# A fused sparse attention and MoE kernel: where the second weight is loaded, scaled and split

## The chip, the cores and the metric

The kernel runs on 1 core of one Trainium2 chip. The metric is the device time of one execution in microseconds (us): before the change 816.15 us, the median of 3 runs (813.92 to 816.83). Engines are named as in the profile: PE multiplies matrices, ACT applies functions and scales, DVE does element-wise work and reductions, POOL gathers, SP starts transfers (as do ACT and POOL). Transfers run on 16 DMA engines.

## The reference

```
scores = q @ k^T / sqrt(64), only where the block mask allows   # batch 4, heads 8, 768 tokens, blocks of 32
attn   = softmax(scores) @ v                                    # neighbours, first and last block, 3 sampled blocks
x      = attn as [3072, 512]
h      = x @ w_in                                               # w_in  [512, 2048]
g      = h * erf(softplus(h))
out    = g @ w_out                                              # w_out [2048, 512]
```

All inputs are float32 but the two MoE weights, which arrive as float64: the kernel gets them as pairs of 32-bit words and makes float32 of them. Block 0 and block 23 attend to everything; they are the "f" units below, the 22 others (two at a time) the "m" units.

## The kernel before

**Weights.** A weight is loaded in pieces of 1024 KB (`load_w`), decoded from the 64-bit form by three DVE instructions (`decode`), and squared and summed by ACT (`square`). From the sums comes a power-of-two scale, one per half of the first weight (`scale_half`) and one per pair of rows of the second (`scale_pair`). With it each 128x512 piece is split into two float16 parts, so that three float16 products give nearly the exact one: ACT writes the upper part (`high`), DVE the rest (`low`), which needs the upper part first. For the first weight PE forms the rest instead, with a diagonal of the scale (`rest`, then `rest_low`, and `rest_out` on ACT). The generator `weights` has 17 steps n=0 to 16: n=0 to 7 decode the first weight, n=8 to 15 the second; step n from 9 on scales pair n-9 of the second weight and splits it, 16 `high` and 16 `low` in all. The instructions of the splits show in the profile as `wo<-wo,sums 128x512`.

**Prologue and loop.** Six attention units run ahead (`for begun in range(FIRST)`), each calling three steps of `weights`; the rest of its steps follow, and then the main loop over 48 groups of 256 feed-forward columns by 256 tokens (plus 3 turns that only finish). Turn m computes a group `h` of 24 products with the first weight (`ff_first`), its logarithms on ACT (`ff_logs`), the values of an earlier attention unit (`po`), the scores of the next unit (`s_m`, or `s_f` for the first and last blocks), the products `o` with the second weight of group m-3, the gate of group m-2 (`s<-s,h`, then two `g`), the maxima (`mx`), `ff_power`, the exponentials (`pf`), `ff_exp` (`s<-s` on ACT), and then `next_queries`, which copies the queries of the next unit to their place (`qm`, two DVE copies), and `behind`, which prepares the values and keys of the next batch (`vmax`, `fold`, `vn_of`, `vraw`, `kr`).

Three buffers hold `h`, so the `h` of turn m+3 waits for the gate of group m, which runs in turn m+2. The scores of a turn need the `qm` of the turn before. Each engine works through its own list of instructions in order. For turns m from 3 on (`held[0] = m >= FF_LAG`) that list has the order in which the calls are written; before, a scheduler places the instructions of PE, ACT and DVE, and `high_priority` moves some ahead. SP's and POOL's stand as written everywhere.

**Loads of the second weight.** ACT issues them. The table `loads` in `weights` names the step after which a piece is loaded; pieces ("o", 4) and ("o", 6) both follow step 7. The program lets a load wait for an earlier transfer that uses the same completion counter, and ACT stands at that load until the earlier one has landed.

Of the kernel before, what the change touches and what calls it, by code (L numbers as in the profile page):

```python
# [2 lines left out]

# [10 lines left out]
ALU = mybir.AluOpType  # L14
# [16 lines left out]
def sparse_attention_moe(ctx: ExitStack, tc: tile.TileContext, qT, kT, v, sampled, w_in, w_out, out):  # L31
# [5 lines left out]
    held, queued = [False], [True]  # L37

    class InOrder:
# [3 lines left out]
        def __getattr__(self, name):  # L43
            call = getattr(self.engine, name)

            def issue(*args, **kwargs):
                done = call(*args, **kwargs)  # L47
                if self.held[0]:
                    tc.keep_in_program_order(done)
                return done  # L50

            return issue

    nc = tc.nc
    pe, act, dve, pool, sp = (
# [7 lines left out]
    NK = DM // P  # L63
# [34 lines left out]
    ones, eye = room[:, :P], room[:, P : 2 * P]  # L98
# [305 lines left out]
    def load_w(key, i):  # L404

        if key == "o" and i >= 12:
            tag, bufs = (("vraw", 1), ("xT", 3), ("xT", 3), ("x", 2))[i - 12]
            rows = w_out[i // 2 * 2 * P :][: 2 * P].bitcast(I32).rearrange("(p n) c -> p n c", n=2)[:, i % 2]
            if tag == "x":
                parts = [mo.tile([P, 512], I32, tag=tag, name=f"raw_{i}_{u}", bufs=bufs) for u in range(2)]  # L410
            elif tag == "vraw":
                parts = [ld.tile([P, H // 2, KT * D], I32, tag=tag, name=f"raw_{i}", bufs=bufs).rearrange("p a b -> p (a b)")[:, :1024]]
            else:
                parts = [mo.tile([P, 1024], I32, tag=tag, name=f"raw_{i}", bufs=bufs)]
            c = 0
            for raw in parts:
                (sp if i == 15 else act).dma_start(raw, rows[:, c : c + raw.shape[1]])
                c += raw.shape[1]
            places[key, i] = parts
            return  # L420
        if key == "i":
            raw = slots(wi, 1 + 2 * i, 4) if i < 8 else slots(wo, 2 * i - 16, 4)
            part, kt = divmod(i // 2, NK)
            sp.dma_start(raw, w_in[kt * P : (kt + 1) * P, part * 1024 : (part + 1) * 1024].bitcast(I32))
        else:
            raw = slots(wo, 2 + 2 * i if i < 8 else 10 + 2 * (i - 8), 4)
            rows = w_out[i * P : (i + 2) * P, :].bitcast(I32).rearrange("(p n) c -> p n c", n=2)
            act.dma_start(raw.rearrange("p (n c) -> p n c", n=2), rows)
        places[key, i] = [raw]

    def decode(key, i):

        first = i + APART[key]
        t = wi if key == "i" else wo
        w32 = t[:, first : first + 2, :].rearrange("p n c -> p (n c)")
        parts = [raw for n in (i, i + 1) for raw in places.pop((key, n), [])]
        mag = mags[(i // 2) % 2]
        c = 0
        for raw in parts:
            w = raw.shape[1] // 2  # L440
            raw = raw.rearrange("p (n w) -> p n w", w=2)
            lo, hi = raw[:, :, 0], raw[:, :, 1]
            m = mag[:, c : c + w]
            dve.tensor_scalar(m, hi, 3, 0x3FFFFFFF, ALU.logical_shift_left, ALU.bitwise_and)
            dve.scalar_tensor_tensor(m, hi, -0x40000000, m, ALU.bitwise_and, ALU.bitwise_or)
            done = w32[:, c : c + w].bitcast(I32)
            dve.scalar_tensor_tensor(done, lo, 29, m, ALU.logical_shift_right, ALU.bitwise_or)
            c += w
# [7 lines left out]
    def halves(key, i):  # L456
        t, t16 = (wi, wi16) if key == "i" else (wo, wo16)
        w32, hi16, lo16 = t[:, i + APART[key], :], t16[:, i, :512], t16[:, i, 512:]
        if key == "i":
            w32 = w32.rearrange("p (n q e) -> p n e q", n=2, e=2)  # L460
            hi16, lo16 = (x.rearrange("p (n e q) -> p n e q", n=2, e=2) for x in (hi16, lo16))
        return w32, hi16, lo16
# [5 lines left out]
    def high(key, i):  # L468
        w32, hi16, _ = halves(key, i)
        act.activation(hi16, w32, AF.Copy, scale=scale_of(key, i))  # L470

    def low(key, i):
        w32, hi16, lo16 = halves(key, i)
        dve.scalar_tensor_tensor(lo16, w32, scale_of(key, i), hi16, ALU.mult, ALU.subtract)

    NP = NF // 2
    eo, so, io = (sums[:, 16 + n * (NP + 2) : 16 + (n + 1) * (NP + 2)] for n in range(3))
    si, ii = so[:, NP:], io[:, NP:]
# [13 lines left out]
    def scale_pair(i):  # L492
        n = i // 2
        total = ps_o.tile([P, DM], F32, tag="o", name=f"total_{i}")[:, :1]
        pe.matmul(total, ones, wsq["o"][:, n : n + 1], start=True, stop=True)
        scale_part(total, n)
# [3 lines left out]

    def scale_half(total, part):
        scale_part(total, NP + part)
        dve.tensor_scalar(diag, eye, si[:, part : part + 1], None, ALU.mult)

    def ratios():
        dve.tensor_reduce(least[:, 0:1], si, AX.X, ALU.min)
# [6 lines left out]
        dve.tensor_tensor(unscale, least[:, 0:1], least[:, 1:2], ALU.mult)  # L513

    rests = {}

    def rest(i):
        rests[i] = ps_o.tile([P, DM], F32, tag="o", name=f"rest_{i}")
        pe.matmul(rests[i], diag, halves("i", i)[0], start=True, stop=False)

    def rest_low(i):
        pe.matmul(rests[i], less16, wi16[:, i, :512], start=False, stop=True)
# [4 lines left out]
    assert NK * NG == NF == 16  # L527

    def weights():
        loads = {5: (("o", 0),), 6: (("o", 2),), 7: (("o", 4), ("o", 6)), 10: (("o", 8),), 11: (("o", 10),)}  # L530
        sum_i = None
        for n in range(17):
            key, i = "io"[n // 8 % 2], n % 8 * 2
            if n in (4, 9):
                with tc.high_priority():
                    scale_half(sum_i, n // 8)
            pair = None
            if 5 <= n < 9:
                pair = 2 * (n - 5)
            if 10 <= n < 14:  # L540
                pair = 2 * (n - 6)
            if pair is not None:
                for part in range(2):
                    rest(pair + part)
                    high("i", pair + part)
            if n < 16:
                decode(key, i)
            if pair is not None:
                for part in range(2):
                    rest_low(pair + part)  # L550
                    rest_out(pair + part)
            if n < 16:
                square(key, i)
            if n >= 9:
                i = 2 * (n - 9)
                scale_pair(i)
                high("o", i)
                high("o", i + 1)
                low("o", i)
                low("o", i + 1)  # L560
            for piece in loads.get(n, ()):
                load_w(*piece)
            if n in (3, 7):
                sum_i = bound_part(n // 4)
            yield
        ratios()

    softs = {}

# [203 lines left out]
    def ff_exp(b, ch, fg):  # L773
        s2 = ffs[b, ch, fg][1]
        act.activation(s2, s2, AF.Exp, scale=-C5)
# [201 lines left out]
    for m in range(len(groups) + FF_LAG):  # L977
        ch, i = divmod(m, NGR)
        held[0] = m >= FF_LAG
        steps = 0  # L980
        if ch < len(until):
            first = until[ch - 1] if ch else FIRST
            steps = int(i in spread[until[ch] - first])
        elif begun < len(units) + PV_LAG:
            steps = 1
        assert steps in (0, 1)
        group = groups[m] if m < len(groups) else None
        last = groups[m - GATE_LAG] if GATE_LAG <= m < len(groups) + GATE_LAG else None
        unit = unit_of(begun) if steps else None
        old = unit_of(begun - PV_LAG) if steps and begun - PV_LAG >= SEEN else None  # L990
        place = seen(old) if old else None
        begun += steps
        if group:
            ff_first(*group)
            ff_logs(*group)
        if place:
            values(*place)
            used_values(place)
        if steps:
            gathers()  # L1000
        if unit:
            scores(unit)
            used_keys(unit)
        if m >= FF_LAG:
            for u in range(CT):
                ff_second(*groups[m - FF_LAG], u)
            for u in range(CT):
                ff_store(*groups[m - FF_LAG], u)
        if last:
            ff_gate(*last)  # L1010
        if open_unit:
            soft_low(open_unit)
        if place:
            norm(*place)
        if unit:
            soft_max(unit)
        if place:
            turn(*place)
        if group:
            ff_power(*group)  # L1020
        if unit:
            soft_exp(unit)
        if group:
            ff_exp(*group)
        open_unit = unit
        if unit:
            next_queries(begun - 1)
            behind(begun - 1)
# [36 lines left out]
```

## Time and profile before

| | |
|---|---|
| median of 3 runs | 816.15 us (813.92 to 816.83) |
| the profiled execution | 814.76 us, span 813.0 us |
| PE busy | 722.7 us (89%) |
| DVE busy | 644.8 us (79%) |
| ACT busy | 603.0 us (74%) |
| granted TensorE clock, mean | 0.960 |

The profile is of one execution. "Span" is the time from its first to its last instruction. A row of a timeline gives the start in us from the beginning of the span, the duration, the engine, the operation, the output and inputs by the program's names, and the shapes; in square brackets stands the idle time of the engine ahead of it and what ended that. The chain of waits is followed back from one point to what released it, so the rows of one chain add up to the time it covers. All instructions pass through one helper, and so all stand at line L47 of the kernel: the names tell them apart. A turn of the loop is found by its `h`: the fourth (m=3) starts at 136.38 us, the next ones at 146.09, 154.23, 162.45, 171.87 and 180.46 us.

### The profile page before, as it was taken

The page shows a single profiled execution, that of the slowest core. Times are in us where ns is not written, and L with a number is a line of the kernel's source. Part 1 is how long each engine was busy: PE and PEld are TensorE (multiplying, and loading weights), DVE is VectorE, ACT ScalarE, POOL GpSimd, SP SyncE. Part 2 cuts the span into 40 slices and gives each one's busy share as a digit, 9 for nine tenths or more (in the row PEclk, how much of TensorE's full clock was granted, in tenths as well). Part 3 has the DMA queues.
Part 4 walks back from the last instruction along what each step waited for, and adds up shares of the span by engine and source line. Part 5 has one row for each costly group of instructions (what it writes and reads, how often), then busy time and mean ns, then how long its engine had stood idle before and what let it go on. Part 6 is the DMA issues. An engine that isn't in the chain of part 4 may idle for free.

```text
span 813.0 us, 26533 instructions
## 1 busy us (share of the span) xinstructions
PE 722.7 (89%) x11136; PEld 507.8 (62%) x11136; DVE 644.8 (79%) x1251; ACT 603.0 (74%) x1035; POOL 198.0 (24%) x382
## 2 busy tenths in 40 slices
PE   2355894979979899999999899999999999999997
PEld 2233563756757577666767577667677776666663
DVE  6685998988869887887778798887888887776664
ACT  2554889777857678787866877878878878777674
POOL 4045530302434231400133233200343310000000
PEclk9867996999999999999999999999999999999999
DMA  9999822986499697843498697744497648312000
GB/s 319 394 232 276 236 88 55 229 203 166 117 238 233 139 230 201 195 122 80 126 184 179 179 228 181 181 101 111 114 201 176 142 122 184 73 27 48 8 27 26
DMA packets 187288, 129.46 MB, mean 159 GB/s; under 512 B 137761, under 2 KB 160929, under 8 KB 185377
## 3 DMA queue, kind: packets, MB, share of 16 engines
q1 hardware_dynamic: 173440, 83.98, 46.3%
q10 hardware_dynamic: 7840, 25.96, 10.0%
q0 software_dynamic: 5888, 17.84, 8.5%
q8 instruction: 87, 1.43, 0.8%
q14 instruction: 33, 0.26, 0.1%
HBM read 82.81 MB, written 12.95 MB: 118 GB/s over the span
## 4 chain that ended last, share of the span: by engine, by line
PE 65%; DVE 13%; DMA 10%; ACT 7%; issue 4%; SPq 0%; ACTq 0%; DVEq 0%
PE h L47 26%; PE o L47 23%; PE s_m L47 7%; PE po_None L47 4%; PE s_f L47 3%; DVE s L47 3%; DMA vbuf<-vtab 3%; DMA wo<-in_w_in_dram 2%; DMA qt<-in_qT_dram 2%; DVE p_m L47 2%; ACT s L47 2%; ACT pf_m L47 2%; ACT x L47 2%; DVE mx_m L47 1%; DMA vtab<-vn 1%
## 5 line engine op out<-in xcount | busy, mean ns | idle before, releaser
L47 PE MATMUL h<-xT,wi 128*128 128x256 f16 x2304 | 274.0, 277 | 20.2 <-DVE s L47 20.1
L47 PEld LDWEIGHTS <-wi 128*128 128x128 f16 x2304 | 228.2, 99 | 71.4 <-issue 13.3
L47 PE MATMUL o<-wo,g 128*128 128x512 f16 x1152 | 266.0, 381 | 1.0 <-issue 0.8
L47 PEld LDWEIGHTS <-g 128*128 128x128 f16 x1152 | 109.9, 98 | 122.4 <-issue 2.9
L47 POOL DMA_INDIRECT vbuf<-vtab,idx x88 | 92.4, 1050 | 370.0 <-PE po_None L47 289.1
L47 ACT ACTIVATE s<-s 128x512 f32<-128x512 f32 x192 | 120.2, 627 | 39.7 <-DVE s L47 30.1
L47 ACT ACTIVATE x<-x 128x512 f32<-128x512 f32 x192 | 120.9, 630 | 5.9
L47 PE MATMUL s_m<-kx,qm 128*64 128x96 f32 (+1 forms) x1408 | 95.1, 245 | 16.2 <-DVE qm L47 11.1
L47 POOL COPY kg<-kx 128x128 f32 x264 | 89.9, 387 | 69.7 <-PE s_m L47 56.8
L47 ACT ACTIVATE pf_m<-s_m,nb_m 128x256 f32<-128x256 f32 x176 | 69.2, 475 | 41.1 <-DVE nb_m L47 40.9
L47 ACT ACTIVATE x<-h,isg 128x512 f32<-128x512 f32 x96 | 65.3, 680 | 31.8 <-PE h L47 31.6
L47 DVE SCALAR_TENSOR_TENSOR s<-x 128x512 f32<-128x512 f32 x96 | 67.8, 706 | 26.2 <-ACT x L47 26.0
L47 DVE SCALAR_TENSOR_TENSOR s<-s,s 128x512 f32<-128x512 f32 x96 | 66.7, 695 | 23.1 <-ACT s L47 19.9
L47 PEld LDWEIGHTS s_m<-kx,qm 128*64 128x64 f32 x1408 | 71.2, 144 | 20.7 <-ACT qm L47 11.0
L47 DVE SCALAR_TENSOR_TENSOR g<-s,sums,g 128x512 f16<-128x512 f32 x96 | 72.2, 752 | 3.4
L47 DVE TENSOR_REDUCE mx_m<-s_m 128x4 f32<-128x1024 f32 x44 | 53.6, 1218 | 20.2 <-PE s_m L47 20.2
L47 PE MATMUL s_m<-kg,qm 128*64 128x96 f32 x704 | 66.5, 256 | 2.5 <-issue 2.4
L47 DVE SCALAR_TENSOR_TENSOR s<-s,h 128x512 f32<-128x512 f32 x96 | 65.3, 681 | 0.5
L47 ACT ACTIVATE s<-x 128x512 f32<-128x512 f32 x96 | 60.5, 630 | 2.9
L47 PE MATMUL po_None<-vbuf,pT_m 128*32 128x65 f16 (+1 forms) x4224 | 45.4, 196 | 7.4 <-issue 2.5
L47 PEld LDWEIGHTS <-pT_m 128*32 128x32 f16 x4224 | 38.6, 94 | 20.6 <-issue 17.0
L47 DVE TENSOR_TENSOR p_m<-pf_m,p_m 128x1024 f16<-128x1024 f32 x38 | 50.3, 1324 | 0.6 <-ACT p_m L47 0.6
(117 smaller groups left out, 681.2 us busy)
## 6 DMA issues: line engine op xcount, KB each, us to landing
vbuf<-vtab SPq DMA_DIRECT2D x80, 195.0 KB
vraw<-in_v_dram ACTq DMA_DIRECT2D x9, 768.0 KB
vbuf<-vtab SPq DMA_DIRECT2D x12, 520.0 KB
wo<-in_w_out_dram ACTq DMA_DIRECT2D x6, 1024.0 KB
qt<-in_qT_dram SPq DMA_DIRECT2D x20, 256.0 KB
vtab<-vn_of SPq DMA_DIRECT2D x13, 390.0 KB
kr<-in_kT_dram ACTq DMA_DIRECT2D x12, 384.0 KB
vbuf<-vtab SPq DMA_DIRECT2D x32, 130.0 KB
```

The costliest lines, as they stand in the source:

```text
L47: done = call(*args, **kwargs)
```

## The change

Four things change. The piece ("o", 6) of the second weight is loaded after the first square of the second weight (step 8), in written order, and no longer after step 7; decoding at step 8 is in written order too. The second half of the first weight gets its scale at step 8, ahead of that decoding, and no longer at step 9. Each half's scale has a diagonal buffer of its own (`diags`), where both used one. And the splits of the second weight leave `weights`: a new function `split_pair` makes two `high` and two `low` at the end of each of the first eight turns of the loop, after `ff_exp` and ahead of `next_queries`. The scales of the pairs stay in `weights`.

```diff
+    @contextmanager
+    def in_order(on=True):
+        was, held[0] = held[0], held[0] or on
+        yield
+        held[0] = was
...
-        dve.tensor_scalar(diag, eye, si[:, part : part + 1], None, ALU.mult)
+        dve.tensor_scalar(diags[part], eye, si[:, part : part + 1], None, ALU.mult)
...
+    diags = diag, line
...
-        pe.matmul(rests[i], diag, halves("i", i)[0], start=True, stop=False)
+        pe.matmul(rests[i], diags[i // (2 * NK)], halves("i", i)[0], start=True, stop=False)
...
-        loads = {5: (("o", 0),), 6: (("o", 2),), 7: (("o", 4), ("o", 6)), 10: (("o", 8),), 11: (("o", 10),)}
+        loads = {5: (("o", 0),), 6: (("o", 2),), 7: (("o", 4),), 10: (("o", 8),), 11: (("o", 10),)}
...
-            if n in (4, 9):
+            if n in (4, 8):
...
-                decode(key, i)
+                with in_order(n == 8):
+                    decode(key, i)
...
             if n >= 9:
-                i = 2 * (n - 9)
-                scale_pair(i)
-                high("o", i)
-                high("o", i + 1)
-                low("o", i)
-                low("o", i + 1)
+                scale_pair(2 * (n - 9))
             for piece in loads.get(n, ()):
                 load_w(*piece)
+            if n == 8:
+                with in_order():
+                    load_w("o", 6)
...
+    def split_pair(fg):
+        for i in (2 * fg, 2 * fg + 1):
+            high("o", i)
+            low("o", i)
...
         if group:
             ff_exp(*group)
+        if m < NP:
+            split_pair(m)
         open_unit = unit
         if unit:
             next_queries(begun - 1)
```

The moved load stands in ACT's list. Before (`qm` are the query copies that follow it, `sq_o` the first square of the second weight):

```order
37 L47 DMA wo<-in_w_out_dram 128x2048
38 L47 ACTIVATE wi<-wi,sums 128x512
39 L47 DMA wo<-in_w_out_dram 128x2048
40 L47 ACTIVATE qm_98<-qt_2_139 64x8x32 x2
41 L47 ACTIVATE wi<-rest_504 128x512
42 L47 ACTIVATE wi<-rest_507 128x512
43 L47 ACTIVATE sq_o_756,sums<-wo 128x1024
```

With the change, from the same place on and then around the load:

```order
37 L47 DMA wo<-in_w_out_dram 128x2048
38 L47 ACTIVATE wi<-wi,sums 128x512
39 L47 ACTIVATE qm_98<-qt_2_139 64x8x32 x2
40 L47 ACTIVATE wi<-rest_504 128x512
41 L47 ACTIVATE wi<-rest_507 128x512
```

```order
 L47 ACTIVATE xT_0_624<-turned 128x2x128
-L47 ACTIVATE pT_m_3_903<-turned 128x2x256
+L47 ACTIVATE pT_m_3_907<-turned 128x2x256
+L47 ACTIVATE sq_o_759,sums<-wo 128x1024
+L47 DMA wo<-in_w_out_dram 128x2048
+L47 ACTIVATE pT_m_3_907<-turned 128x2x256
```

The load no longer stands ahead of the copies; it follows the first `sq_o`, which itself comes later.

DVE's list in turn m=3, before:

```order
211 L47 TENSOR_SCALAR nb_m_8_2021<-mx_m_8_2019 128x4
212 L47 TENSOR_TENSOR x_0_5_2023<-xf_5_2017,x_0_5_2023 128x256
213 L47 SCALAR_TENSOR_TENSOR s_0_0_3_2027<-x_0_3_1842 128x512
214 L47 SCALAR_TENSOR_TENSOR s_0_0_3_2027<-s_0_0_3_1846,s_0_0_3_2027 128x512
215 L47 COPY qm_98<-qt_4_1556 64x8x32 x2
216 L47 SCALAR_TENSOR_TENSOR s_0_0_2_1813<-s_0_0_2_1813,h_0_2_1774 128x512
```

and with the change:

```order
204 L47 TENSOR_SCALAR nb_m_8_2001<-mx_m_8_1999 128x4
205 L47 TENSOR_TENSOR x_0_5_2003<-xf_5_1997,x_0_5_2003 128x256
206 L47 SCALAR_TENSOR_TENSOR s_0_0_3_2007<-x_0_3_1822 128x512
207 L47 SCALAR_TENSOR_TENSOR s_0_0_3_2007<-s_0_0_3_1826,s_0_0_3_2007 128x512
208 L47 SCALAR_TENSOR_TENSOR wo<-wo,sums 128x512 x2
209 L47 COPY qm_98<-qt_4_1528 64x8x32 x2
210 L47 SCALAR_TENSOR_TENSOR s_0_0_2_1789<-s_0_0_2_1789,h_0_2_1750 128x512
```

Two `low` now stand between `ff_power` and the copies of `qm`; the gate of the next turn follows the copies as it did.

ACT's list in turn m=3, before:

```order
133 L47 ACTIVATE pf_m_8_2030<-s_m_8_1971,nb_m_8_2021 128x256 x4
134 L47 ACTIVATE p_m_8_2035<-pf_m_8_2030 128x4x256
135 L47 ACTIVATE s_0_0_3_2027<-s_0_0_3_2027 128x512
136 L47 DMA vraw_1_2043<-in_v_dram 128x1536
137 L47 ACTIVATE x_0_4_2070<-h_0_4_2045,isg_1480 128x512
```

and with the change:

```order
126 L47 ACTIVATE pf_m_8_2010<-s_m_8_1951,nb_m_8_2001 128x256 x4
127 L47 ACTIVATE p_m_8_2015<-pf_m_8_2010 128x4x256
128 L47 ACTIVATE s_0_0_3_2007<-s_0_0_3_2007 128x512
129 L47 ACTIVATE wo<-wo,sums 128x512 x2
130 L47 DMA vraw_1_2027<-in_v_dram 128x1536
131 L47 ACTIVATE x_0_4_2054<-h_0_4_2029,isg_1448 128x512
```

Two `high` stand behind the exponential of `s` and ahead of the logarithms of the next turn. The turns m=4 to m=6 look the same on both engines. Up to the fourth `h`, 12 `high` and 12 `low` stand in the lists before, and 6 of each with the change. SP's and POOL's lists keep their order.

More of the change, by code (lines that the diff above doesn't have):

```diff
@@ L1 @@
 import math
-from contextlib import ExitStack
+from contextlib import ExitStack, contextmanager
 import concourse.bass as bass
```

## The prediction

> **What bounds the kernel now.** I read the busy time per engine in the stretches between the `h` groups of TensorE first (each `h` group opens one turn of the main loop), then the chain of waits up to the fourth of them, then the rows of DVE and ACT inside the turns m=3 to m=6. The profiled execution took 814.76 us around a span of 813.0 us; the median of the runs shown, 816.15, lies 1.39 above it. Of this kernel a change under 0.5% (4.1 us) can't be told from none.
>
> The stretches (start:end, length, then busy time of each engine, granted clock, DMA share, GB/s); the second to the fifth are the turns m=3 to m=6:
> ```profile
> 58.90:67.30 8.40, 2.42 (x116) 1.63 (x110) 4.90 (x9) 0.02 (x1) 7.93 (x17) 0.83 1.01 305
> ...
> 124.00:136.40 12.40, 1.80 (x9) 1.46 (x10) 10.34 (x31) 12.40 (x25) 0.00 (x0) 0.58 0.18 40
> 136.40:146.10 9.70, 9.70 (x181) 6.97 (x182) 9.52 (x18) 8.47 (x16) 2.14 (x2) 0.83 0.38 92
> 146.10:154.20 8.10, 8.10 (x181) 6.15 (x180) 7.52 (x16) 6.85 (x14) 2.30 (x2) 1.00 0.93 232
> 154.20:162.50 8.30, 8.30 (x182) 6.28 (x181) 7.76 (x28) 5.42 (x9) 2.67 (x3) 1.00 1.08 247
> 162.50:171.90 9.40, 7.60 (x138) 5.03 (x137) 7.57 (x15) 6.49 (x13) 0.83 (x1) 1.00 0.62 157
> ```
> Before the fourth `h` ACT is the bound: 12.40 us busy out of 12.40, with PE at 1.80. In the turns m=4 and m=5 PE is (8.10 of 8.10, 8.30 of 8.30), but DVE follows at 7.52 and 7.76: little room is left on it. The chain of waits into the fourth `h` shows what ACT and DVE do there:
> ```profile
> 124.78 1.22 ACT wo L47 x2
> ...
> 129.29 1.22 ACT wo L47 x2
> ...
> 134.41 0.98 DVE wo L47 x2
> ...
> 135.65 0.69 DVE s L47
> ...
> 136.38 4.35 PE h L47 x24
> ```
> The halves of the second weight (`wo`) stand on that chain with 1.22 + 1.22 + 0.98 = 3.42 us. Up to that point, from 90 us on, there are 12 of each:
> ```profile
> L47 ACT ACTIVATE wo<-wo,sums 128x512 f16<-128x512 f32 x12 | 8.2, 728 | 0.0
> ...
> L47 DVE SCALAR_TENSOR_TENSOR wo<-wo,sums 128x512 f16<-128x512 f32 x12 | 8.8, 746 | 1.2 <-ACT wo L47 1.0
> ```
>
> **Part 1: halves that leave the stretch before the fourth `h`.** Of the 12 pairs of instructions, 6 stay (turns m=0 to 2) and 6 go into later turns. That frees 6 x 8.2/12 = 4.1 us on ACT and 6 x 8.8/12 = 4.4 us on DVE; the chain holds 3.42 us of them directly. ACT is full and DVE is 10.34 of 12.40, so the freed ACT time should show nearly whole: I take **-4.0 us**. Bounds: -1.5 (only part of the 3.42 is gained, since `h` waits for a gate that DVE forms behind other work) and -7.
>
> **Part 2: the load that moves behind the first square, and the earlier second scale.** The fourth big load of the second weight was issued by ACT at a point where it had to wait (ACT's row first, then two of the chain of waits):
> ```profile
> 67.31 0.84 ACT L47 ACTIVATE qm<-qt 64x256 f32<-64x256 f32 x2 [8.39 <-DMA wo<-in_w_out_dram]
> ...
> 63.07 15.67 DMA vbuf<-vtab
> ...
> 78.78 0.95 PE po_None L47 x94
> ```
> Copies of queries, weight halves and exponentials stood behind it for 8.39 us. Yet the chain there runs through a transfer (`vbuf`, 15.67 us) whose end at 78.78 releases PE; it does not run through ACT, and after it PE is the bound for 40 us (15.00 busy of 15.00 between 95 and 110):
> ```profile
> 95.00:110.00 15.00, 15.00 (x183) 9.72 (x182) 14.79 (x32) 12.34 (x25) 5.51 (x8) 0.89 0.47 123
> 110.00:124.00 14.00, 13.81 (x133) 9.33 (x130) 11.69 (x28) 12.70 (x23) 5.13 (x8) 1.00 0.55 153
> ```
> So the hold is covered by that landing and by PE's work, and I count its removal as 0. If the cover is gone it is worth up to -8.39. It can also turn against the change: the load now starts later, and its decoding (and all scales behind it) with it; ACT's row of 12.70 busy in 14.00 says 1.3 us of slack for that, so the other end is +1.5. The second diagonal buffer and the scale one step earlier take no instruction more; 0.
>
> **Part 3: the halves in the turns m=3 to m=7.** Here the order is kept as written. A turn gets two ACT halves behind the exponential of `s`, and two DVE halves that wait for them, ahead of the two copies of `qm`. DVE works its rows in order, so the copies, and behind them the gate (`s<-s,h`) of the next turn, queue behind the halves. DVE's rows, m=3 and m=4:
> ```profile
> 143.84 1.21 DVE L47 TENSOR_REDUCE mx_m<-s_m 128x4 f32<-128x1024 f32 x1
> ...
> 146.35 0.69 DVE L47 SCALAR_TENSOR_TENSOR s<-s,s 128x512 f32<-128x512 f32 x1
> 146.96 0.58 DVE L47 COPY qm<-qt 64x256 f32<-64x256 f32 x2
> 147.58 0.69 DVE L47 SCALAR_TENSOR_TENSOR s<-s,h 128x512 f32<-128x512 f32 x1
> ...
> 151.74 1.22 DVE L47 TENSOR_REDUCE mx_m<-s_m 128x4 f32<-128x1024 f32 x1 [0.29 <-PE s_m L47]
> ...
> 155.36 1.93 DVE L47 TENSOR_REDUCE vmax<-vraw 128x1 f32<-128x384 f32 x4
> ...
> 160.32 0.68 DVE L47 SCALAR_TENSOR_TENSOR s<-s,h 128x512 f32<-128x512 f32 x1
> ...
> 164.19 1.21 DVE L47 TENSOR_REDUCE mx_m<-s_m 128x4 f32<-128x1024 f32 x1
> ...
> 169.42 1.15 DVE L47 SCALAR_TENSOR_TENSOR vn_of<-vraw,s_v,vn_of 128x384 f16<-128x384 f32 x2 [1.65 <-ACT vn_of L47]
> 170.48 0.68 DVE L47 SCALAR_TENSOR_TENSOR s<-s,h 128x512 f32<-128x512 f32 x1
> ```
> and ACT's, DVE's and PE's that close the walk:
> ```profile
> 155.83 0.61 ACT L47 ACTIVATE s<-s 128x512 f32<-128x512 f32 x1
> ...
> 168.27 0.61 ACT L47 ACTIVATE s<-s 128x512 f32<-128x512 f32 x1
> 168.79 1.10 ACT L47 ACTIVATE vn_of<-vraw,s_v 128x384 f16<-128x384 f32 x2
> ...
> 177.51 0.61 ACT L47 ACTIVATE s<-s 128x512 f32<-128x512 f32 x1
> ...
> 174.53 0.94 DVE L47 TENSOR_REDUCE mx_f<-s_f 128x1 f32<-128x768 f32 x1
> ...
> 179.73 0.68 DVE L47 SCALAR_TENSOR_TENSOR s<-s,h 128x512 f32<-128x512 f32 x1
> ...
> 180.46 4.45 PE L47 MATMUL h<-xT,wi 128*128 128x256 f16 x24 [3.21 <-DVE s L47]
> ```
> Pieces, start to start. From `mx` to the exponential: 155.83 - 151.74 = 4.09. The exponential holds ACT 168.79 - 168.27 = 0.52. Two ACT halves 1.22 (the chain's own row), then the second DVE half 0.75, then the copies 147.58 - 146.96 = 0.62. So the copies end 4.09 + 0.52 + 1.22 + 0.75 + 0.62 = 7.20 after `mx`, where before they ended 147.58 - 143.84 = 3.74 after it.
> - `mx` m=3 to m=4: 7.20, then gate to `mx` 151.74 - 147.58 - 0.29 = 3.87, is 11.07; before 151.74 - 143.84 = 7.90. **+3.2**. (PE needs only some 8.1 for a turn, so it waits for `qm`, and `mx` for DVE.)
> - m=4 to m=5: 7.20, then the maxima of the values 160.32 - 155.36 = 4.96, then 164.19 - 160.32 = 3.87, is 16.03; before 12.45. **+3.6**.
> - m=5 to m=6 (`mx_f`): 7.20, the value halves 170.48 - 169.42 = 1.06, then 174.53 - 170.48 = 4.05, is 12.31; before 10.34. **+2.0**. The wait of 1.65 in the row of `vn_of` covers part of it.
> - `mx_f` to the gate that frees the buffer of the ninth `h`: 177.51 - 174.53 = 2.98, then 0.52 + 1.22 + 0.75 + 1.06 = 3.55, is 6.53; before 179.73 - 174.53 = 5.20. **+1.3**.
>
> Sum 10.1. Off it go 0.3 for halves that stood before `mx` in m=3 of the kernel before, and 0.3 for rows that overlap by some 0.07 each. **+9.5 us** at the ninth `h`; bounds +7.5 (the first DVE half and the copies fall into waits) and +11. The two halves of m=7 I take at **0**:
> ```profile
> 184.65 0.63 ACT L47 ACTIVATE s<-s 128x512 f32<-128x512 f32 x1 [2.30 <-DVE s L47]
> ...
> 189.71 2.78 PE L47 MATMUL h<-xT,wi 128*128 128x256 f16 x24
> ```
> ACT has 2.30 idle there; with the cover gone it is +1.2.
>
> **Sum.** -4.0 + 0 + 9.5 + 0 = +5.5: 820.3 for the profiled execution, **821.6** by the median. What comes after the ninth `h` is paced by the loop itself, so I let the shift stay. By the bounds -7 + 7.5 = +0.5 (816.7) to -1.5 + 1.5 + 11 + 1.2 = +12.2 (828.4); the likeliest case's own range is 817.5 to 825.5.
>
> **Rivals.**
> A. The loop swallows the halves. PE is the bound in the turns, and 2 x 0.75 on DVE's 7.52 is 9.0, only 0.9 above PE's 8.10; if `qm` were not held up by ACT, m=3 to m=6 would cost 4 x 0.9 at most or, with DVE's waits (1.65 in one row) filled, about nothing, and -4.0 would be left: **812.2**. Against it: the halves wait for the exponential, which is ACT's last of the turn. It decides if the copies still end within 4.1 us of `mx`: 3.74, and the 0.4 between DVE's 7.90 and PE's 8.30.
> B. Not slower, by the start. The 8.39 us that ACT stood still are truly on the path (a queue of ACT that is full until 136.40 and hands every microsecond on): -8.39 - 4.0 + 9.5 = -2.9, **813.3**. For it: ACT's 12.40 of 12.40. Against it: PE's 15.00 of 15.00 in between. It decides once the fourth `h` starts over 9.5 us earlier, before 126.9; with part of A added it would be faster by more than 0.5%.
> C. Given back later. There is a long wait at the change of batch:
> ```profile
> 221.52 6.84 DMA pT_f<-p_f
> ...
> 231.63 3.89 issue
> ```
> If what ends it does not move with the loop, up to all of the +5.5 goes into 6.84 + 3.89 us: **816** to 817. Against it: that transfer is issued by a turn of the loop, which is late by the same amount.
> D. A colder clock. After a wait of 9.25 us PE's 24 products of `h` took 4.35 us, and 4.45 after one of 3.21, with 2.78 when it had not waited; part 3 makes PE wait for `qm` or the gate by what its 8.1 of work is short of 11.07, 16.03 and 12.31: 3, 8 and 4 us. If two or three groups on the path pay 1.7 more (4.45 - 2.78): 821.6 + 3.4 to 5.1, **826**. Against it: in those turns DVE sets the pace, and PE's 8.1 at half speed would only partly exceed 11 to 16.
>
> The Trainium skill, "TensorE: Matmul & The Clock Gate", Part 1 (what's actually happening), has the array fall to half rate after an idle window of about 3.4 us and come back after a busy one as long, and calls the window free-running. The trace agrees with the ratio (4.45 to 2.78) and shows it after an idle of 3.21; by that rule alone the waits of 8 and 4 us leave the array cold each time, and the time would be that of rival D with two groups, 825.0.
>
> That the change does nothing of what it says is out: the rows of instructions have moved as told above.
>
> **Chances.** Forecast 0.54 (of it three parts in four above 820.2, the rest within 0.5%). A 0.14 (two thirds below 812.1), B 0.13 (half), C 0.08 (within), D 0.11 (above). Slower: 0.54 x 0.75 + 0.11 = 0.52. Faster: 0.14 x 0.65 + 0.13 x 0.5 = 0.16. Within: 0.32. The range that leaves out 2 in 10 takes in B and most of D: 812 to 826.5.
>
> **What would show it.** In the profile of the changed kernel: the fourth `h` some 4 us earlier (132.4), with the `wo` rows gone from the chain ahead of it but for those of m=0 to 2; no ACT wait of 8 us on a load near 60 us, and `po` still released by the landing of `vbuf`; the distance from `mx` to `mx` at 11 and 16 us, with `qm` some 7.2 behind `mx` and PE waiting for `qm` in m=4 and m=5; the ninth `h` near 186; from there on equal turns. Wrong would be: a fourth `h` over 9 us earlier (B), turns of 8 to 9 us with two halves in them (A), or the shift at 186 gone by 250 (C).

## The result and the profile after

The changed kernel took **822.7 us** (median of 5 runs, 822.03 to 828.58) against 816.15 before: a ratio of **1.012, 95% interval 1.0083 to 1.0157**. The forecast was 821.6, slower. The profiled execution was the longest of the five (828.58, span 826.7), so its distances inside a turn are read here, and not its end. It is 13.8 us longer than the profiled execution of the kernel before (814.76); the four others of the changed kernel (822.03 to 822.89) have no profile. All ratios leave out one execution of 2543.03 us, in the experiment with the halves where their inputs are ready; every other lies between 813 and 844 us.

Busy time by stretch, in the changed kernel (columns as before; the second to the fifth row are the turns m=3 to m=6):

```profile
124.00:134.00 10.00, 1.06 (x5) 0.92 (x6) 8.36 (x29) 10.00 (x21) 0.00 (x0) 0.58 0.30 66
134.00:144.60 10.60, 10.60 (x180) 7.33 (x181) 7.03 (x14) 6.42 (x13) 1.86 (x2) 0.75 0.28 73
144.60:154.10 9.50, 8.24 (x181) 6.18 (x180) 7.15 (x14) 6.96 (x12) 1.97 (x2) 1.00 0.79 196
154.10:168.00 13.90, 11.16 (x182) 8.18 (x181) 11.04 (x34) 7.46 (x13) 3.05 (x3) 0.75 0.73 150
168.00:182.70 14.70, 9.00 (x137) 5.66 (x136) 12.05 (x23) 9.31 (x17) 1.06 (x1) 0.88 0.61 135
```

Two turns have grown to 13.90 and 14.70 us (8.30 and 9.40 before), and in neither of them is any engine full: what sets the time is a chain, not a load. DVE's rows show it:

```profile
142.15 1.22 DVE L47 TENSOR_REDUCE mx_m<-s_m 128x4 f32<-128x1024 f32 x1 [1.00 <-PE s_m L47]
...
147.50 1.41 DVE L47 SCALAR_TENSOR_TENSOR wo<-wo,sums 128x512 f16<-128x512 f32 x2 [2.13 <-ACT wo L47]
148.83 0.58 DVE L47 COPY qm<-qt 64x256 f32<-64x256 f32 x2
...
153.24 1.21 DVE L47 TENSOR_REDUCE mx_m<-s_m 128x4 f32<-128x1024 f32 x1
...
158.58 1.41 DVE L47 SCALAR_TENSOR_TENSOR wo<-wo,sums 128x512 f16<-128x512 f32 x2 [2.26 <-ACT wo L47]
...
169.26 1.21 DVE L47 TENSOR_REDUCE mx_m<-s_m 128x4 f32<-128x1024 f32 x1
...
182.10 0.94 DVE L47 TENSOR_REDUCE mx_f<-s_f 128x1 f32<-128x768 f32 x1
...
188.74 0.68 DVE L47 SCALAR_TENSOR_TENSOR s<-s,h 128x512 f32<-128x512 f32 x1
```

From `mx` to `mx` it is 11.09, 16.02 and 12.84 us, and 6.64 from `mx_f` to the gate, where it was 7.90, 12.45, 10.34 and 5.20. DVE stands 2.13 and 2.26 us for ACT's halves, with the query copies and the next gate behind it. PE's rows show who waits for that in turn:

```profile
133.94 5.30 PE L47 MATMUL h<-xT,wi 128*128 128x256 f16 x24 [7.43 <-DVE s L47]
...
149.56 0.39 PE L47 MATMUL s_m<-kx,qm 128*64 128x96 f32 x4 [1.25 <-DVE qm L47]
...
160.63 0.59 PE L47 MATMUL s_m<-kx,qm 128*64 128x96 f32 x4 [2.73 <-DVE qm L47]
...
177.37 2.90 PE L47 MATMUL s_f<-kx,qm 128*128 128x512 f32 x4 [5.70 <-DVE qm L47]
...
189.47 2.78 PE L47 MATMUL h<-xT,wi 128*128 128x256 f16 x24 [1.34 <-DVE s L47]
```

The fourth `h` starts 2.44 us earlier than before (133.94 against 136.38), the ninth 9.01 later (189.47 against 180.46). Between the two the change costs 55.53 - 44.08 = 11.45 us.

Ahead of the loop ACT no longer stands 8.39 us at the load. It stands elsewhere. The load and the first square in the kernel before:

```profile
66.93 0.33 ACTq L47 DMA_DIRECT2D wo<-in_w_out_dram  x1
...
69.28 1.06 ACT L47 ACTIVATE sq_o<-wo 128x1024 bf16<-128x1024 f32 x1
```

and ACT in the changed kernel:

```profile
72.25 0.84 ACT L47 ACTIVATE qm<-qt 64x256 f32<-64x256 f32 x2 [5.41 <-PE s_m L47]
...
77.68 0.60 ACT L47 ACTIVATE pT_m<-turned 128x512 f16<-128x512 f32 x1 [4.59 <-PE turned L47]
...
86.99 1.06 ACT L47 ACTIVATE sq_o<-wo 128x1024 bf16<-128x1024 f32 x1 [4.00 <-DVE wo L47]
87.00 0.33 ACTq L47 DMA_DIRECT2D wo<-in_w_out_dram  x1
```

Waits of 5.41, 4.59 and 4.00 us stand there (before, one of 4.98 stood at 81.75 besides the 8.39), the load is issued at 87.00 instead of 66.93, and the first square of the second weight (`sq_o`) starts at 86.99 instead of 69.28. This was not in the forecast, and the first experiments turn on it.

### The profile page after: what moved, and what is told of

It is laid out like the page before. It is cut to its first block, busy times and chain, and to the rows that moved or that the text cites. A ratio compares the mean times of both kernels' runs of the same rounds, so it can differ in the third digit from the quotient of the medians.

```text
span 826.7 us, 26534 instructions
## 1 busy us (share of the span) xinstructions
PE 727.7 (88%) x11136; PEld 510.4 (62%) x11136; DVE 645.1 (78%) x1251; ACT 601.6 (73%) x1035; POOL 196.3 (24%) x382
## 4 chain that ended last, share of the span: by engine, by line
PE 66%; DVE 15%; DMA 7%; ACT 7%; issue 4%; SPq 1%; ACTq 0%; DVEq 0%
PE h L47 25%; PE o L47 24%; PE s_m L47 8%; PE po_None L47 4%; DMA qt<-in_qT_dram 3%; DVE s L47 2%; PE s_f L47 2%; ACT x L47 2%; DVE g L47 2%; DMA vbuf<-vtab 2%; ACT s L47 2%; DVE mx_m L47 2%; DVE room L47 1%; ACT pf_m L47 1%; DVE vn_of L47 1%
## 5 line engine op out<-in xcount | busy, mean ns | idle before, releaser
L47 POOL DMA_INDIRECT vbuf<-vtab,idx x88 | 96.5, 1097 | 369.8 <-PE po_None L47 297.5
L47 PE MATMUL s_m<-kx,qm 128*64 128x96 f32 (+1 forms) x1408 | 98.2, 249 | 17.4 <-DVE qm L47 15.1
L47 POOL COPY kg<-kx 128x128 f32 x264 | 83.5, 362 | 73.7 <-PE s_m L47 58.0
L47 PEld LDWEIGHTS s_m<-kx,qm 128*64 128x64 f32 x1408 | 74.0, 147 | 24.9 <-ACT qm L47 10.5
L47 PE MATMUL s_m<-kg,qm 128*64 128x96 f32 x704 | 69.0, 260 | 7.3 <-issue 7.1
L47 PEld LDWEIGHTS s_m<-kg,qm 128*64 128x64 f32 x704 | 47.7, 147 | 9.5 <-issue 9.0
```

## The experiments

All ratios are against the kernel before, run beside the experiment. It took 824 to 826 us there, 8 to 9 more than beside the change, so times are compared within one set of runs and distances within a profile. There were four sets: the first four runs; then the kernel before, the change, the old load with the halves ahead and the scale alone; then the three with decoding free; then the last. A start compared across sets carries what runs differ by, up to some 3 us (136.38 and 133.48 in two profiles of the kernel before); the loop of the same two differs by 1.8 (44.08 and 45.91). "Start" is the fourth `h`; "loop" is from the fourth `h` to the ninth.

**The halves stay, the rest of the change is made.** Against the changed kernel:

```diff
-                scale_pair(2 * (n - 9))
+                i = 2 * (n - 9)
+                scale_pair(i)
+                high("o", i)
+                high("o", i + 1)
+                low("o", i)
+                low("o", i + 1)
...
-        if m < NP:
-            split_pair(m)
```

> Edit: the moved load, the earlier second scale and the second diagonal buffer alone; the halves of the second weight stay where they were. Theory (the loss is the chain that the halves make in turns m=3 to m=6; the load is worth nothing): 816, ratio 0.997 to 1.003, fourth h between 135 and 137.5. Rival 1 (ACT's stand of 8.39 us was on the path): 808 to 812, fourth h before 131. Rival 2 (the later load and its decoding cost what was lost): 819 to 822.

Measured: 1.0102 (1.003 to 1.0173), start at 137.99. Neither the theory nor the rival of a gain holds: the part that I had counted at nothing is a loss by itself, about as large as rival 2 had it.

**The halves go into the loop, the rest stays as before.** Against the kernel before:

```diff
+        if m < NP:
+            split_pair(m)
...
-                high("o", i)
-                high("o", i + 1)
-                low("o", i)
-                low("o", i + 1)
```

> Edit: the halves formed in the loop alone; load, scale and diagonal as before. Theory: as slow as the whole change, 821 to 823 (fourth h 2.5 to 4 us earlier, mx to mx 11.1 and 16.0 in m=3 to m=5). Rival 2 (the load carries the loss): 812 to 816. Rival 1 (the load was the gain of the start): the fourth h stays at 136 and the time is 825 or more.

Measured: 1.0137 (1.0045 to 1.0228), start at 128.93, `mx` to `mx` 11.09 and 17.31. As slow as the whole change, by the loop; and the start comes 3 to 9 us earlier than in the kernels with load and scale edited (137.99 above, 133.94 in the change, 132.10 and 132.40 in the two runs that follow). So the halves do gain at the start, and the other edits take it back. The second distance is 1.3 above the 16.02 of the change because a pair of copies of `qm` took 1.87 us there (0.58 in most turns).

**The halves behind the query copies.** Against the changed kernel:

```diff
-        if m < NP:
-            split_pair(m)
...
             behind(begun - 1)
+        if m < NP:
+            split_pair(m)
```

> Edit: the whole change, with the two pairs of halves behind the query copies and behind the next batch's work. Theory (DVE stands for ACT's halves, whatever is behind them): mx to mx 10.4 in m=3 to m=4 (4.61 + 1.22 + 0.75 + 3.87), 14.1 in m=4 to m=5, so 3 to 3.5 us of some 10 come back: 819 to 820. Rival (the late query copies are what costs, since PE waits for them): the whole loss of the loop comes back, 812 to 814.

Measured: 1.0068 (1.0033 to 1.0102). DVE's rows:

```profile
141.60 1.23 DVE L47 TENSOR_REDUCE mx_m<-s_m 128x4 f32<-128x1024 f32 x1 [2.35 <-PE s_m L47]
...
144.74 0.58 DVE L47 COPY qm<-qt 64x256 f32<-64x256 f32 x2
146.96 1.41 DVE L47 SCALAR_TENSOR_TENSOR wo<-wo,sums 128x512 f16<-128x512 f32 x2 [1.63 <-ACT wo L47]
...
152.07 1.22 DVE L47 TENSOR_REDUCE mx_m<-s_m 128x4 f32<-128x1024 f32 x1
```

The copies are in time (3.14 after `mx`), and the turn still takes 10.47 us, 10.4 expected, with DVE standing 1.63 for ACT. The late copies are thus worth 0.6 us in this turn (10.47 against 11.09); the wait in DVE's list is what costs. In the next turn DVE has the maxima of the values to do before the halves, does not stand, and the distance is 13.68 instead of 16.02. Loop 52.81.

**The halves where their inputs are ready.** Against the changed kernel:

```diff
             ff_first(*group)
+            if m < NP:
+                high("o", 2 * m)
+                high("o", 2 * m + 1)
             ff_logs(*group)
...
             ff_gate(*last)
+        if m < NP:
+            low("o", 2 * m)
+            low("o", 2 * m + 1)
...
-        if m < NP:
-            split_pair(m)
```

> Edit: the whole change, with ACT's halves at the head of the turn (ahead of the logarithms) and DVE's behind the gate, so that DVE finds them ready. Theory: only DVE's work of 1.4 per turn is added, mx to mx 9.0 and 13.9 instead of 11.1 and 16.0; the loop costs 3 to 4 instead of 10, the start stays 2.5 to 4 earlier: 814.5 to 817. Rival (the work as such is too much for a turn that has 0.6 of DVE to spare, wherever it stands): 820 to 823.

Measured: 1.0036 (1.0006 to 1.0066). DVE's rows:

```profile
141.24 1.22 DVE L47 TENSOR_REDUCE mx_m<-s_m 128x4 f32<-128x1024 f32 x1 [2.35 <-PE s_m L47]
...
146.90 1.41 DVE L47 SCALAR_TENSOR_TENSOR wo<-wo,sums 128x512 f16<-128x512 f32 x2
...
150.11 1.21 DVE L47 TENSOR_REDUCE mx_m<-s_m 128x4 f32<-128x1024 f32 x1
```

The same two instructions, with no wait in front: `mx` to `mx` is 8.87 and then 13.68 (9.0 and 13.9 expected). Loop 49.71: the same work costs 3.8 us and not 10.1 (by the 45.91 and 56.04 of the next two runs) when it stands where its input is ready. The ratio is above what was expected (814.5 to 817 is 0.998 to 1.001 of 816.15) and below the rival's (820 is 1.005), and its interval reaches both; the start is only 1.4 earlier than the 133.48 of the next run, not 2.5 to 4.

**The kernel before, and the change, once more on one chip.** No edit.

> Edit: none, the kernel before, for a profile of it on the same chip as the runs beside it (the kernel before took 825.0 in the median beside the first four experiments, 816.2 beside the change). All theories: turns as in the first profile, mx to mx 7.9 and 12.4 in m=3 to m=5; fourth h at 134 to 137; the difference between the chips lies outside m=3 to m=7.

Measured: 820.27 (one execution), start at 133.48, `mx` to `mx` 8.14 and 12.55, loop 45.91. The loop of the first profile was 44.08, so the difference does not lie outside m=3 to m=7 alone.

> Edit: none, the changed kernel once more. Theory: slower than the kernel before by 5 to 8 on the same chip (ratio 1.006 to 1.010), mx to mx 11.1 and 16.0 in m=3 to m=5. Rival (the change did worse on one chip by its transfers alone): ratio within 0.996 to 1.003, same turns.

Measured: 1.0157 (1.0096 to 1.0217), start at 133.71, `mx` to `mx` 11.09 and 16.01, loop 56.04. These two distances of the first profile return to 0.01 us. On this chip the start is not earlier at all (+0.23), so the 2.44 between the two first profiles came in part from the runs. The ratio is above the one expected: I had left out that loss at the start.

**The halves ahead, with the load and the scale of before.** The edit of the fourth experiment, against the kernel before.

> Edit: the loop halves where the fourth experiment had them (ACT's at the head of the turn, DVE's behind the gate), with load, scale and diagonal as before the change. Theory (the later load takes back 3 to 5 of what the start gains; the halves so placed cost some 4 in the loop): fourth h 5 to 7.5 earlier than in the kernel before, time 1 to 4 below it (ratio 0.995 to 0.999). Rival (the load is worth nothing by itself): fourth h 2.5 to 4.5 earlier and the time that of the fourth experiment, ratio 1.002 to 1.005.

Measured: 1.0003 (0.9968 to 1.0037), start at 130.63, loop 49.13. It is 2.85 earlier at the start than the kernel before and 3.22 longer in the loop: nothing left. The loop was near what was expected; the start was not (5 to 7.5 expected, 2.5 to 4.5 by the rival), and the time 1 to 4 below the kernel before did not come. The interval takes in a part of both forecasts.

**The earlier second scale alone.** It comes with its own diagonal and with decoding at step 8 in written order; "scale alone" below means the three together. Against the kernel before:

```diff
+    diags = diag, line
...
-            if n in (4, 9):
+            if n in (4, 8):
...
-                decode(key, i)
+                with in_order(n == 8):
+                    decode(key, i)
```

> Edit: the earlier second scale, the second diagonal buffer and decoding at step 8 in written order, with load and halves as before. Theory (what the first experiment lost comes from the load, issued some 20 us later): ratio 0.997 to 1.003, fourth h as in the kernel before. Rival (decoding in written order, queued behind an attention unit, is what costs): ratio 1.006 to 1.01, as in the first experiment.

Measured: 1.0112 (1.0073 to 1.0151), start at 141.05. The theory (the late load) falls: the load is back in its place, and the loss is there. The first experiment differs from this run in the place of the load alone: ACT does not stand at it there and stands 7.07 us here, and the ratios are 1.0102 and 1.0112, a difference of 0.001 with an uncertainty of some 0.008, over two sets. In DVE's rows of the kernel before (first) and of the changed one (second), on one chip, one sees what stands where:

```profile
61.01 0.74 DVE L47 TENSOR_SCALAR room<-wo 128x1024 int32<-128x1024 int32 x1 [4.11 <-DMA wo<-in_w_out_dram]
...
63.05 1.22 DVE L47 SCALAR_TENSOR_TENSOR wo<-wo,room 128x1024 int32<-128x1024 int32 x1
```

```profile
65.21 0.69 DVE L47 TENSOR_SCALAR room<-wo 128x1024 int32<-128x1024 int32 x1 [1.47 <-DMA wo<-in_w_out_dram]
65.94 1.23 DVE L47 SCALAR_TENSOR_TENSOR room<-wo,room 128x1024 int32<-128x1024 int32 x1
...
71.87 1.23 DVE L47 TENSOR_REDUCE mx_m<-s_m 128x4 f32<-128x1024 f32 x1 [3.97 <-PE s_m L47]
...
80.43 0.16 DVE L47 TENSOR_SCALAR sums<-allm_wi 128x1 int32<-128x1 int32 x1 [3.38 <-PE allm_wi L47]
...
81.01 0.69 DVE L47 TENSOR_SCALAR room<-wo 128x1024 int32<-128x1024 int32 x1
...
82.41 1.22 DVE L47 SCALAR_TENSOR_TENSOR room<-wo,room 128x1024 int32<-128x1024 int32 x1
...
84.60 1.22 DVE L47 SCALAR_TENSOR_TENSOR wo<-wo,room 128x1024 int32<-128x1024 int32 x1
```

Decoding ends its first piece (`wo<-wo,room`) at 64 before and at 86 after. The rows at 65.21 and 65.94 are of the second piece, which waits for the transfer that DVE waits for at 67.22 in the kernel before; the first piece, whose data landed near 60 in both, begins only at 81.01. It stands behind the second scale, which waits until PE has summed the squares of the first weight (3.38, to 80.43). The hole that DVE had in this stretch was what decoding was done in. The busy times of both kernels say the same (before, then changed):

```profile
60.00:85.00 25.00, 15.33 (x274) 9.79 (x274) 14.96 (x26) 12.94 (x26) 15.34 (x30) 0.80 0.89 261
...
109.00:122.00 13.00, 12.16 (x120) 8.48 (x119) 12.43 (x31) 13.00 (x25) 5.31 (x8) 1.00 0.59 165
```

```profile
60.00:85.00 25.00, 19.35 (x415) 13.87 (x412) 11.79 (x27) 11.68 (x25) 14.95 (x36) 0.73 0.78 223
...
109.00:122.00 13.00, 13.00 (x133) 8.26 (x130) 13.00 (x29) 9.10 (x17) 7.02 (x8) 1.00 0.62 165
```

3.2 us of DVE's and 1.3 of ACT's work leave a stretch that had room (60 to 85) for one that hasn't. From 109 to 122 DVE and PE are then full, and ACT, full before, waits (9.10 of 13.00); the squares that it should do there come after 122, the last at 123.05 instead of 116.92, in the stretch that bounds the fourth `h`.

**The whole change, but decoding is free again.** Against the changed kernel:

```diff
-                with in_order(n == 8):
-                    decode(key, i)
+                decode(key, i)
```

> Edit: the whole change, but decoding at step 8 is left to the scheduler, which puts the first decoding of the second weight ahead of the second scale again (the load stays behind the first square, and with it moves some 15 us earlier). Theory (the 3 to 5 us that the start lost are the decoding held behind the second scale): first square of the second weight near 70 and not 86, fourth h 3 to 5 us earlier than in the changed kernel on the same chip, loop as there; ratio 1.006 to 1.011 where the change had 1.016. Rival (the load's lateness is what costs, or the scale): fourth h as in the changed kernel, ratio 1.013 to 1.018.

Measured: 1.0097 (1.0067 to 1.0127), first square at 65.00, start at 130.09, loop 55.99. The start is 3.62 earlier than in the changed kernel and the loop the same, as the theory had it; but the 133.71 is of another set, on another chip, so the size of the first number is known no better than starts repeat (up to 3 us). With the early scale alone, decoding is back in its old place, so it was the written order that held it behind that scale. Written order without the early scale was not run. The load goes out at 70.63 here, at the end of a wait of ACT of 4.92.

**The same, with the halves ahead.**

> Edit: the same, with the halves in the loop placed as in the fourth experiment (ACT's at the head of the turn, DVE's behind the gate). Theory: the start gains 4, the loop costs 4: ratio 0.996 to 1.001, as with the old load (1.0003). Rival (ACT no longer standing at the load is worth its 8 us once decoding is not held up): ratio 0.985 to 0.993.

Measured: 0.9994 (0.9963 to 1.0024), start at 132.41, loop 47.83. Decoding is not late, and the 8 us don't come. But ACT still stands at the load, now in its new place behind the first square. ACT's rows:

```profile
71.51 0.34 ACTq L47 DMA_DIRECT2D wo<-in_w_out_dram  x1
71.95 1.57 ACT L47 ACTIVATE pf_m<-s_m,nb_m 128x256 f32<-128x256 f32 x4 [5.86 <-DMA vbuf<-vtab]
```

The chain of waits shows what the load waited for, a transfer into `vbuf` (the kernel before waited for one of `wo`):

```profile
61.67 9.81 DMA vbuf<-vtab
...
71.51 0.34 ACTq L47
```

The 8.39 us have become 5.86 and not 0, so this run does not say what an ACT that never stands there would be worth; in the pair with late decoding it was worth nothing that could be seen (1.0102 and 1.0112). Nor is the start what was expected: it is 1.1 earlier than the 133.48 of another set, not 4, and no earlier than with late decoding and the halves ahead (132.10), while the ratio is lower (0.9994 against 1.0036) by as much as its uncertainty. This is the least time of all variants, and not to be told from the kernel before.

**DVE's halves on POOL.** The run before, with

```diff
+    def low_pool(key, i):
+        w32, hi16, lo16 = halves(key, i)
+        pool.tensor_scalar(w32, w32, scale_of(key, i), None, ALU.mult)
+        pool.tensor_tensor(lo16, w32, hi16, ALU.subtract)
```

for `low` in m=3 to m=7.

> Edit: the same as the run before it, with DVE's halves of m=3 to m=7 on POOL, as two instructions each (scale in place, then subtract). Theory (what is left of the loss in the loop is DVE's 1.4 us per turn): mx to mx back to 7.9 to 8.3 and 12.4 to 12.8 in m=3 to m=5, ratio 0.992 to 0.997. Rival (POOL's work slows DVE's or holds up gathers): turns of 9 and more, ratio 1.000 to 1.008.

Measured: 1.0058 (1.0034 to 1.0083), `mx` to `mx` 9.53 and 16.58. The rival was right: the work left DVE, and DVE became slower. POOL's row and DVE's of the same moments:

```profile
148.94 2.32 POOL L47 TENSOR_SCALAR wo<-wo,sums 128x512 f32<-128x512 f32 x1
```

```profile
148.20 0.79 DVE L47 TENSOR_SCALAR nb_m<-mx_m 128x4 f32<-128x4 f32 x1
...
150.85 1.81 DVE L47 COPY qm<-qt 64x256 f32<-64x256 f32 x2
```

These two took 0.17 and 0.58 in the kernel before (the copies in most turns); POOL's form took 1.57 us at 157.71.

**Three pairs late, five early.** Against the kernel before: the generator splits only pairs 0 to 4, and the turns m=6 to m=8 each one pair more, placed as in the fourth experiment.

```diff
+                if i < 10:
+                    high("o", i)
...
+            if 6 <= m < 9:
+                high("o", 2 * m - 2)
+                high("o", 2 * m - 1)
...
+        if 6 <= m < 9:
+            low("o", 2 * m - 2)
+            low("o", 2 * m - 1)
```

> Edit: load, scale and diagonal as before the change; five pairs of halves stay ahead of the loop, the last three are formed in turns m=6, 7 and 8, ACT's at the head of the turn and DVE's behind the gate (the products need them in m=8, 9 and 10). Theory (what leaves the start is worth 0.7 a half, what stands ready in a turn costs DVE's 1.4, less where a turn has no unit or waits): fourth h 1 to 2 earlier, m=6 to m=8 together 1 longer, ratio 0.996 to 1.000. Rival (halves in the loop cost more than they bring wherever they stand): ratio 1.002 to 1.006.

Measured: 1.001 (0.9982 to 1.0038), start at 134.26, loop 48.11. No gain, and the start not earlier than the 133.48 of the kernel before in another set of runs. Whether the theory or the rival is right about it can't be told at this size.

The runs side by side (us; the distances come from one profile of each):

| run | ratio | start | `mx` to `mx`, m=3 to 5 | loop |
|---|---|---|---|---|
| before (same set as the change's second run) | 1 | 133.48 | 8.14, 12.55 | 45.91 |
| change | 1.0157 | 133.71 | 11.09, 16.01 | 56.04 |
| load and scale alone | 1.0102 | 137.99 | 8.12, 12.37 | 46.57 |
| scale alone | 1.0112 | 141.05 | 8.17, 12.53 | 45.62 |
| halves alone | 1.0137 | 128.93 | 11.09, 17.31 | 57.80 |
| change, decoding free | 1.0097 | 130.09 | 11.08, 16.02 | 55.99 |
| change, halves behind the copies | 1.0068 | 132.40 | 10.47, 13.68 | 52.81 |
| change, halves ahead | 1.0036 | 132.10 | 8.87, 13.68 | 49.71 |
| old load, halves ahead | 1.0003 | 130.63 | 8.86, 13.69 | 49.13 |
| decoding free, halves ahead | 0.9994 | 132.41 | 8.97, 13.69 | 47.83 |
| the same, on POOL | 1.0058 | 128.64 | 9.53, 16.58 | 53.18 |

No version beats the kernel before beyond what was measured as its uncertainty (some 0.3%).

## Why the prediction was right, and where it was not

- **Part 1 (-4.0 at the fourth `h`)** was right for the halves alone: 133.48 - 128.93 = 4.55 earlier with them alone, 3.39 with decoding free, 2.85 with the old load and the halves ahead. Only the last is of one set; with decoding free and the halves ahead it was 1.07, and 4.84 in the same kernel with POOL's halves.
- **Part 2 (0, at worst +1.5)** was wrong. I costed the load and passed over the scale: "the scale one step earlier takes no instruction more; 0". It takes none, but decoding was tied behind it, and the cover that it lost was DVE's hole near 60 to 80 us. Its price at the fourth `h` is 3.6 us (133.71 against 130.09, two sets), or 3.1 against the old load with the halves ahead in the same set (130.63); with the halves in their old place 4.5 to 7.6. Between the two kernels with the halves ahead (132.10 and 132.41) the start shows none of it, so one profile each gives the size only roughly; as time it is 1.0112 for the scale alone. For the load, the 0 is not contradicted: with decoding late, taking ACT's stand away changed the ratio by 0.001 (uncertainty 0.008). With decoding free ACT stood there again, for 4.92 and 5.86 us, so an ACT freed for good was not measured.
- **Part 3 (+9.5)** was right, and row by row: 11.07, 16.03, 12.31 and 6.53 in the prediction, 11.09, 16.02, 12.84 and 6.64 in the profile. The 0.5 in the third is one pair of copies that took 1.22 and not 0.58. The loop cost 56.04 - 45.91 = 10.1 on one chip and 11.45 between the first two profiles, above the upper bound of 11; of the 11.45 the four distances make 10.7, and 0.75 lies between the fourth `h` and the first `mx` (8.21 against 7.46). As the experiment behind the copies shows, what matters in it is that DVE's list stands for ACT, with the gate behind it; the late copies, which I named first, are worth 0.6 in m=3.
- **m=7 (0, at most +1.2)** is not settled by a run of its own; from the ninth to the twelfth `h` the change loses 2.4 more against the kernel before of its set (10.36 to 12.78), but only 0.5 between the first two profiles (22.53 against 22.04), and others lose there too: the old load with the halves ahead 2.43 and the scale alone about 2.8, which has no halves there. The loop that goes on from here has 96 groups, not 48: the page of the kernel before counts 2304 products of `h`, 24 a group.
- **The sum (+5.5)** came near the measured +6.55 partly by luck: the start gained 0 to 2.4 and not 4.0, the loop lost a little more than forecast, and in the second set the change is 13.2 us slower, not 5.5. With Part 2 at its measured size the sum would be -4.0 + 3.6 + 9.5 = +9.1, which lies between the +6.55 and +13.2 of the two sets. What makes the two differ was not found; their turns m=3 to m=5 don't, and the profiled executions don't either (13.8 longer in the first set, 14.9 in the second). The +6.55 stands on four executions without a profile.
- **Rivals.** A (the loop swallows the halves) fell with turns of 11 and 16 us. B (the freed 8.39 is on the path) fell with the fourth `h` at most 2.4 earlier. C (given back later) fell in the profiles: 12.7 us late at 373 us in the second set, against 12.8 at the twelfth `h`; in the first, 11.3 at 374 us, against 9.0 at the ninth. D (a colder clock) is half right: the clock did fall in the grown turns (granted 0.75 in 154.10 to 168.00), and PE took 3.68 us for the scores of m=5, with 1.94 before. But `mx` followed `mx` after 16.02, what DVE's walk gives without it. The chain of waits below does run through PE, yet the exponential that it releases starts 0.34 after `nb`, and 0.26 in the kernel before: PE's loss costs 0.1 there. So the turns came out without the 3.4 us of the 825.0. The ratio 4.45 to 2.78 that I read as half rate is 1.6, and the granted clock over the 4.45 at 180.46 was 0.62 in the mean; 0.50 stands over the group that took 5.30 (133.94 in the changed kernel).
- **A reading.** In the first rows of the prediction the turns m=3 to m=6 are the third to the sixth, not the second to the fifth; nothing hangs on it.

The rows of PE in the chain of the changed kernel:

```profile
160.63 3.68 PE s_m L47 x48
164.31 3.84 PE o L47 x12
168.16 2.63 PE h L47 x24
```

## What to carry to other kernels

A piece of work that is moved into a loop costs, besides its duration, the time from its place in an in-order list to the moment its input is ready: two instructions of 0.7 us cost 3.0 to 3.5 us a turn behind a wait, and 0.7 to 1.1 where the input was there. An edit that adds no instruction can still cost when it ties one to a later one: look for what the idle stretch of the profile was used for before counting a reordering at nothing. And a long wait that is taken away (8.39 us here) need not be worth its length: in the changed kernel waits of 5.41, 4.59 and 4.00 us stood in its place, and the fourth `h` came 2.4 earlier or not at all.

## What was not expected of the hardware

DVE and POOL slow each other. In the changed kernel the copies of `qm` at 176.00 took 1.22 us (0.58 in other turns) while POOL copied keys:

```profile
175.71 1.06 POOL L47 COPY kx<-kr 128x768 f32<-128x768 f32 x1 [14.09 <-DMA kr<-in_kT_dram]
```

```profile
176.00 1.22 DVE L47 COPY qm<-qt 64x256 f32<-64x256 f32 x2
```

POOL's copy took 0.83 us at 160.49 and 170.83 in the kernel before. The Trainium skill, "SBUF — State Buffer", "Who interferes with whom", says that copies and `tensor_scalar` on DVE can need a port pair that POOL also uses, and that whoever is first has it for the whole instruction. The rows agree for copies and `tensor_scalar` (`qm` and `nb` above), but with the halves on POOL another form grew too: `s<-s,s`, with two inputs, took 0.98 us at 149.95 and 0.69 in the kernel before. That both sides grow (by 0.64 and by 0.23) goes with two short copies that come between POOL's work, but no run separates that.

PE's clock fell after some waits and not after others of about the same length: 24 products of `h` took 4.45 us behind a wait of 2.05 (load and scale alone) and of 2.68 (decoding free, halves ahead), both at a granted clock of 0.62, but 2.78 at 1.00 behind one of 2.32 (halves on POOL). So the length of the last wait alone does not decide it in these runs.

```profile
278.72 4.45 PE L47 MATMUL h<-xT,wi 128*128 128x256 f16 x24 [2.05 <-DVE s L47]
```

```profile
180.24 4.45 PE L47 MATMUL h<-xT,wi 128*128 128x256 f16 x24 [2.68 <-DVE s L47]
```

```profile
181.82 2.78 PE L47 MATMUL h<-xT,wi 128*128 128x256 f16 x24 [2.32 <-DVE s L47]
```
